# Conv units of a fused causal-convolution and ELU-MLP kernel, rearranged as 64-row tiles in two halves with output rounds in between

## The chip, the cores and the metric

The kernel runs on one core of one Trainium2 chip. Its time is device microseconds of that core, the median of several executions. A ratio is the mean time of one kernel's runs over the mean time of the other's in the same rounds, so it is not quite the ratio of the medians that stand beside it. Intervals are 95% intervals.

Engines are named as the profile does: PE is TensorE's matmul part, PEld its weight load, DVE is VectorE, ACT is ScalarE, POOL is GpSimd.

## The reference, cut to what matters

```python
# x: (8, 4096, 192), weight: (8 heads, 7 taps), moe_w_in: (192, 2048), moe_w_out: (2048, 192)
w   = softmax(weight, axis=-1)                          # per head
att[b, s, h, :] = sum_k w[h, k] * x_pad[b, s + k, h, :] # causal, 24 channels per head
h   = att.reshape(32768, 192) @ moe_w_in
g   = where(h > 0, h, exp(min(h, 0)) - 1)               # ELU
out = g @ moe_w_out
```

## The kernel before: the parts that matter here

32768 tokens are cut into 32 supertiles of 1024 tokens. A supertile has 16 steps; a step ("h" below) computes 128 columns of the hidden layer for 1024 tokens. A half has 8 steps, and it also holds one **conv unit** (four heads of a coming supertile) and 64 **rounds** of the output product of the supertile before. I number the steps of a half 0 to 7.

```python
HALF_STEPS = (10, 10, 6, 6, 10, 11, 11)   # rounds placed behind steps 7, 0, 1, 2, 3, 4, 5 of a half
CONV_AT = ((4, 1, 1), (12, 2, 0))         # a conv unit in step 4 of each half
...
H = psum("H", [P, 3, 2 * GS])             # three slots of two PSUM banks, taken in turn by steps and conv units
ops = psum("ops", [P, 2, GS])             # accumulates the output rounds of a half
...
# TensorE, conv unit m: full-array matmuls, 118 rows of x against a 118 x 112 band of weights
for gr in range(2):
    W(s_x[s % NXB][gr], x_need[s, gr])    # x has landed
W(s_z, z_need[s])
k = slot_of_conv[m]
wait_slot(k)                              # whoever had this slot of H has been read
for q in range(HU):                       # 4 heads
    h = HU * u + q
    ins = pe.matmul(H[0:CW, k % 3, 256 * q : 256 * q + UC],
                    Tm[0:KW, h, :] if s else Tk[0:KW, :, h],
                    xg[0:KW, s % NXB, :, CPH * h : CPH * (h + 1)].rearrange("p w (j i) -> p j w i", j=3),
                    start=True, stop=True)
ins.then_inc(s_cv)
...
# TensorE, a step n: 64-row tiles, three matmuls in each of two row tiles
wait_slot(k)
for j in range(3):
    for r in range(2):
        ins = pe.matmul(H[:, k % 3, GS * r : GS * (r + 1)],
                        w_in[HP * r : HP * (r + 1), j, FC * q : FC * (q + 1)],
                        att[HP * r : HP * (r + 1), s % 2, j, 0:GS],
                        start=(j == 0), stop=(j == 2), tile_position=(HP * r, 0))
ins.then_inc(s_h)
...
# TensorE, a round r: two matmuls, also in 64-row tiles; in the second half of the rounds the
# row tiles swap the two banks of ops (a wait on s_swap stands there)
...
# per step, for each of its two token groups: ScalarE exp(H) -> E; GpSimd clamps E to at most 1;
# VectorE gT = max(E - 1, H), which also frees the slot of H (s_tt)
# ScalarE in the order of the program: exp of step 4, conv eviction, exp of step 5,
# output eviction (ops -> osb, 768 columns), exp of step 6, ...
```

So every step needs a slot of H, and the slot goes round: step n waits until VectorE has finished with what was there three takings ago. In a half the takings are steps 0 to 4, the conv unit, steps 5 to 7. Step 5 therefore takes the slot of step 3, the conv unit that of step 2, and step 7 the conv unit's.

## Time and profile before

| | before |
|---|---|
| time, median of 3 runs | 762.6 us (761.82 to 762.93) |
| span of the profiled execution | 761.0 us |
| a half (8 steps, 1 conv unit, 64 rounds), steady state | 11.287 us |
| start to start of VectorE ops in the steps that wait for it | 0.598 us |

The period of a half is read from the trace: it is the distance between the first w_in matmuls of step 1 in consecutive halves (median over 52 halves; 11.284 to 11.288 in all of them).

From the page of the kernel before, the busy table and the chain of work that ended last:

```profile
PE 749.1 (98%) x11609; PEld 507.6 (67%) x11612; DVE 636.1 (84%) x1033; ACT 639.4 (84%) x1155; POOL 668.8 (88%) x1110
...
PE 95%; DVE 2%; DMA 1%; POOL 1%; ACT 0%; issue 0%; SPq 0%
```

Read alone, these two lines say that TensorE is the limit and nothing else matters. The Trainium skill warns about the first of them (Perfetto Trace Analysis, Tensor Engine Instruction): the end that the profiler gives for a TensorE instruction is estimated, not observed. This trace fits that: almost every w_in matmul is drawn as 376 ns (the rest as 377 to 387) but the next pair starts 216 ns after it, so bars overlap and a matmul that starts 40 or 100 ns late leaves no idle time in the table. Waits of TensorE have to be looked for in the starts.

The timeline of the kernel before, one half, without the other engines' lines (start and duration in us, engine, line, operation, tiles, count). L490 is a step, L519 are rounds, L466 is the conv unit:

```profile
300.26 0.82 PE L490 MATMUL H<-att,w_in 64*128 64x512 bf16 x6
300.92 0.99 PE L519 MATMUL ops<-w_out,gT 64*128 64x192 f16 x20
301.74 0.81 PE L490 MATMUL H<-att,w_in 64*128 64x512 bf16 x6
302.39 0.58 PE L519 MATMUL ops<-w_out,gT 64*128 64x192 f16 x10
302.89 0.62 PE L466 MATMUL H<-xg,Tm 118*112 118x240 bf16 x4
303.44 0.67 PE L519 MATMUL ops<-w_out,gT 64*128 64x192 f16 x12
...
304.80 1.09 ACT L373 ACTIVATE E<-H 128x512 f32<-128x512 f32 x2 [0.26 <-PE H L490]
...
305.77 0.82 ACT L354 ACTIVATE osb<-ops 128x768 f32<-128x768 f32 x1
...
306.46 3.10 ACT L373 ACTIVATE E<-H 128x512 f32<-128x512 f32 x6
```

Ten rounds take 301.74 - 300.92 = 0.82 us, so a round takes 82 ns. The five rounds before conv take 302.89 - 302.39 = 0.50 us where five rounds need 0.41, and the four conv matmuls take 303.44 - 302.89 = 0.55 us where four times 101 ns (240 columns, the distance inside the unit) is 0.40. That excess, 0.24 us, is what the change aims at. ScalarE's exponential of step 5 (304.80) waits for TensorE.

The timeline of VectorE alone around step 3 of the same half (window 300.7 to 303.2 us; a row starts with its first instruction that reaches into the window):

```profile
300.12 3.67 DVE L416 SCALAR_TENSOR_TENSOR gT<-E,H 128x512 f16<-128x512 f32 x6
```

Six ops without a gap: five distances of 598 ns and one duration of 0.68 us. The last of them is the second op of step 3. It ends at 303.789 us, and step 5, which takes that slot, starts at 303.950 (all starts and ends to the nanosecond are in the trace): 161 ns later. In steps 1, 2 and 3 the same distance is 57 ns in nearly every half, and never less than 56. So 56 to 57 ns is what a held start looks like, and step 5 had 105 ns to spare.

From the table of waits of the kernel before (from 60 to 740 us; us in total, times, longest):

```profile
DVE gT L416 <- POOL E L323: 78.1, 120, 1.2
ACT E L373 <- PE H L490: 66.9, 181, 0.5
```

ScalarE waits for TensorE in part of the steps.

### The profile page before, as it was taken

To read this page: it belongs to the slowest core of one execution; us is meant where nothing else is said; L and a number is where in the kernel's file an instruction comes from. 1 tells how busy PE (TensorE), PEld (TensorE's weight loads), DVE (VectorE), ACT (ScalarE), POOL (GpSimd) and SP (SyncE) were. 2 spreads that over 40 slices of the span, in tenths; PEclk is the share of its full clock that TensorE was granted. 3 is DMA by queue.
4 is the path that set the end of the run, shared out by engine and by line. 5 is a ranking of instruction groups with operands and counts; after the bars stand their busy time and mean duration, and the time that the engine had idled before them with its cause. 6 is when DMAs were issued, how large, how long until landed. Compare 5 with 4: busy or idle time off the path is not lost.

```text
span 761.0 us, 27449 instructions
## 1 busy us (share of the span) xinstructions
PE 749.1 (98%) x11609; PEld 507.6 (67%) x11612; DVE 636.1 (84%) x1033; ACT 639.4 (84%) x1155; POOL 668.8 (88%) x1110
## 2 busy tenths in 40 slices
PE   8899999999999999999999999999999999999997
PEld 3256666666666666676666666666666666667666
DVE  2588888889889889889888888988988988988993
ACT  1588888888888888888888888888888888888882
POOL 3799999899989999989989999989998999998892
PEclk9999999999999999999999999999999999999999
DMA  5845645424654533555542554442454653353212
GB/s 102 132 58 92 92 59 92 84 51 85 92 64 87 91 53 75 93 77 73 92 65 63 92 92 59 91 89 48 84 92 68 84 91 58 71 92 77 46 44 65
DMA packets 135499, 59.31 MB, mean 78 GB/s; under 512 B 101680, under 2 KB 134576, under 8 KB 135376
## 3 DMA queue, kind: packets, MB, share of 16 engines
q1 hardware_dynamic: 90112, 39.68, 23.5%
q0 software_dynamic: 44992, 17.67, 21.4%
q8 instruction: 91, 1.49, 0.8%
q14 instruction: 32, 0.26, 0.1%
q10 hardware_dynamic: 272, 0.20, 0.1%
HBM read 34.80 MB, written 25.45 MB: 79 GB/s over the span
## 4 chain that ended last, share of the span: by engine, by line
PE 95%; DVE 2%; DMA 1%; POOL 1%; ACT 0%; issue 0%; SPq 0%
PE H L490 44%; PE ops L519 44%; PE H L466 5%; DVE gT L416 1%; PE ops L448 1%; POOL E L323 1%; PE H L519 1%; DMA conv_band<-wprb 1%; DMA wq<-in_weight_dram 0%; DMA Tk<-conv_band 0%; ACT E L373 0%; POOL xg L270 0%; POOL w_out L311 0%; ACT osb L354 0%; DVE osb L427 0%
## 5 line engine op out<-in xcount | busy, mean ns | idle before, releaser
L416 DVE SCALAR_TENSOR_TENSOR gT<-E,H 128x512 f16<-128x512 f32 x1024 | 630.5, 682 | 98.9 <-POOL E L323 91.2
L323 POOL TENSOR_SCALAR E<-E 128x512 f32<-128x512 f32 x1024 | 605.1, 614 | 65.9 <-ACT E L373 63.3
L373 ACT ACTIVATE E<-H 128x512 f32<-128x512 f32 x1024 | 546.1, 604 | 95.7 <-PE H L490 82.1
L519 PEld LDWEIGHTS ops<-w_out,gT 64*128 64x128 f16 x8064 | 342.4, 94 | 114.3 <-ACT osb L354 10.8
L519 PE MATMUL ops<-w_out,gT 64*128 64x192 f16 x8064 | 414.5, 243 | 0.9 <-DVE gT L416 0.9
L490 PE MATMUL H<-att,w_in 64*128 64x512 bf16 x3072 | 407.0, 377 | 2.9 <-DVE gT L416 2.8
L490 PEld LDWEIGHTS H<-att,w_in 64*128 64x128 bf16 x3072 | 129.4, 94 | 105.5 <-DVE gT L416 7.2
L366 ACT ACTIVATE csb<-H 112x960 bf16<-112x960 f32 x63 | 61.4, 974 | 10.2 <-PE H L466 10.2
L270 POOL DMA_DIRECT2D xg<-in_x_dram x65 | 59.4, 914 | 6.0 <-DVE csb L406 5.9
L354 ACT ACTIVATE osb<-ops 128x768 f32<-128x768 f32 x63 | 51.5, 817 | 5.1 <-PE ops L519 5.1
L466 PE MATMUL H<-xg,Tm 118*112 118x240 bf16 x248 | 38.2, 277 | 0.7 <-DVE gT L416 0.6
L466 PEld LDWEIGHTS H<-xg,Tm 118*112 118x112 bf16 x248 | 23.7, 129 | 11.4 <-issue 10.8
L448 PE MATMUL ops<-zw 128*128 128x512 bf16 x89 | 25.3, 423 | 1.9 <-DVE zw L384 1.5
L448 PEld LDWEIGHTS ops<-zw 128*128 128x128 bf16 x92 | 9.0, 108 | 15.8 <-issue 9.2
L406 DVE CAST csb<-H 112x960 bf16<-112x960 f32 x1 | 1.2, 1158 | 10.2 <-PE H L466 10.2
L427 DVE COPY osb<-H 128x384 f32<-128x384 f32 x1 | 0.6, 558 | 8.9 <-PE H L519 8.9
L519 PE MATMUL H<-w_out,gT 64*128 64x192 f16 x128 | 5.6, 243 | 0.1
L519 PEld LDWEIGHTS H<-w_out,gT 64*128 64x128 f16 x128 | 5.2, 94 | 0.3 <-PE H L519 0.3
L302 POOL DMA_DIRECT2D w_in<-w_in x1 | 0.7, 682 | 5.3 <-DMA w_in<-in_moe_w_in_dram 5.3
L346 ACT ACTIVATE osb<-H 128x384 f32<-128x384 f32 x1 | 0.5, 491 | 4.7 <-PE H L519 4.7
L288 POOL DMA_DIRECT2D w_in<-in_moe_w_in_dram x6 | 3.5, 598 | 0.9 <-DMA att<-csb 0.9
L466 PE MATMUL H<-xg,Tk 118*112 118x240 bf16 x8 | 2.0, 394 | 1.7 <-DMA Tk<-conv_band 1.7
(20 smaller groups left out, 12.0 us busy)
## 6 DMA issues: line engine op xcount, KB each, us to landing
out_dram<-osb SPq DMA_DIRECT2D x127, 192.0 KB, 3.7
xg<-in_x_dram POOLq DMA_DIRECT2D x62, 240.0 KB, 5.3
w_in<-in_moe_w_in_dram POOLq DMA_DIRECT2D x6, 128.0 KB, 5.2
w_out<-in_moe_w_out_dram POOLq DMA_DIRECT2D x1, 768.0 KB, 7.9
att<-csb SPq DMA_TRANSPOSE x32, 5.8
xg<-in_x_dram POOLq DMA_DIRECT2D x2, 192.0 KB, 4.6
w_in<-w_in POOLq DMA_DIRECT2D x1, 384.0 KB, 4.8
w_in<-w_in SPq DMA_DIRECT2D x1, 384.0 KB, 4.2
```

Source lines behind the costliest of these rows:

```text
L270: g.dma_start(xg[0:rows, b, 2 * w0 + gr : 2 * w1 : 2, :], src).then_inc(s_x[b][gr], 16)
L288: g.dma_start(w_in[0:HP, j, c0:c1], bass.AP(tensor=moe_w_in.tensor, offset=8 * j * FF + c0, ap=[[CPH * FF, HEADS], [FF, 8], [1, c1 - c0]], ...
L323: g.tensor_scalar(out=E[:, n % NE, u, :], in0=E[:, n % NE, u, :], scalar1=1.0, scalar2=0.0, op0=ALU.min, op1=ALU.max,).then_inc(s_clp)
L354: a.activation(osb[:, b, :, :, :].rearrange("p g k d -> p g (k d)"), ops[:, :, 0 : 2 * D], ACT.Copy,).then_inc(s_oev)
L366: a.activation(*conv_evac(W, m), ACT.Copy).then_inc(s_ce)
L373: a.activation(E[:, n % NE, u, :], H[:, k, GS * u : GS * (u + 1)], ACT.Exp).then_inc(s_exp)
L406: v.tensor_copy(*conv_evac(W, 1)).then_inc(s_cd)
L416: v.scalar_tensor_tensor(out=gT[:, s % NG3, q, u, :], in0=E[:, n % NE, u, :], scalar=1.0, in1=H[:, slot_of_pair[n] % 3, GS * u : GS * (u + ...
L448: pe.matmul(ops[:, 0, :], zw[:, 0:P], zw[:, 0:GS], start=True, stop=True)
L466: ins = pe.matmul(H[0:CW, k % 3, 256 * q : 256 * q + UC], Tm[0:KW, h, :] if s else Tk[0:KW, :, h], xg[0:KW, s % NXB, :, CPH * h : CPH * (h ...
L490: ins = pe.matmul(H[:, k % 3, GS * r : GS * (r + 1)], w_in[HP * r : HP * (r + 1), j, FC * q : FC * (q + 1)], att[HP * r : HP * (r + 1), s ...
L519: ins = pe.matmul(acc[:, g, D * kb : D * (kb + 1)], gT[HP * rt : HP * (rt + 1), t % NG3, q, g, t0 : t0 + P], w_out[HP * rt : HP * (rt + 1) ...
```

## The change

Its intent: the conv matmuls use the whole array, everything around them uses 64-row tiles. If the conv unit runs in 64-row tiles too, TensorE need not change its mode twice a unit. Two row tiles may not access the same PSUM bank at a time (the Trainium skill, TensorEngine Tiling (Array Packing), Gotcha 1), so in the first half of a unit row tile 0 takes two heads and row tile 1 the other two, and in the second half they swap. A wait on TensorE's own semaphore stands between the halves, and four output rounds are put there to hide it.

```diff
+            cuts = (r0, r0 + 3, r0 + 7, r1) if convs else (r0, r1)
+            for part, (a, b) in enumerate(zip(cuts, cuts[1:])):
+                order.append(("o", t, half, a, b))
+                for k, u in convs:
+                    if part < 2:
+                        conv_at(k, u, part)
 ...
+                    if part == 0:
+                        (the waits for the band, x, the zeros and the slot, as before)
+                    else:
+                        if 2 <= m <= 3:
+                            warm(WARM[2])
+                        W(s_cswap, 2 * m + 2)
-                    for q in range(HU):
-                        h = HU * u + q
-                        ins = pe.matmul(H[0:CW, k % 3, 256 * q : 256 * q + UC],
-                            Tm[0:KW, h, :] if s else Tk[0:KW, :, h], xg[0:KW, ...],
-                            start=True, stop=True)
-                    ins.then_inc(s_cv)
+                    for q in range(2):
+                        for rt in range(2):
+                            hq = 2 * (rt ^ part) + q
+                            h = HU * u + hq
+                            rows = slice(HP * rt, HP + (KW - HP) * rt)      # 64 and 54 rows
+                            ins = pe.matmul(H[0:CW, k % 3, 256 * hq : 256 * hq + UC],
+                                Tm[rows, h, :] if s else Tk[rows, :, h], xg[rows, ...],
+                                start=(part == 0 and q == 0), stop=(part == 1 and q == 1),
+                                tile_position=(HP * rt, 0))
+                            if q == 1 and part == 0:
+                                ins.then_inc(s_cswap)
+                            elif q == 1:
+                                ins.then_inc(s_cv)
```

(Calls are drawn together and the arguments of xg are cut; the counts in the other engines' waits on s_cv double.)

More of the change, by code (lines that the diff above doesn't have):

```diff
@@ L84, in bass_lightweight_conv__then__act_elu_kernel, with conv_at @@
     last_slot = None
-    def conv_at(s, g):
-        m = 2 * s + g
-        slot_of_conv[m] = take_slot(("c", m))
-        order.append(("c", m))
-    for g in range(2):
-        conv_at(0, g)
+    def conv_at(s, u, part):
+        m = 2 * s + u
+        if part == 0:
+            slot_of_conv[m] = take_slot(("c", m))
+        order.append(("c", m, part))
+    for part in range(2):
+        for u in range(2):
+            conv_at(0, u, part)
     rounds_at = {}
@@ L109, in bass_lightweight_conv__then__act_elu_kernel @@
         else:
-            convs = [(s + ahead, g) for at, ahead, g in CONV_AT if at == i and n < NP]
-        convs = [(k, g) for k, g in convs if k < NS]
+            convs = [(s + ahead, u) for at, ahead, u in CONV_AT if at == i and n < NP]
+        convs = [(k, u) for k, u in convs if k < NS]
         if n in rounds_at:
@@ L115, in bass_lightweight_conv__then__act_elu_kernel @@
                 last_slot = take_slot(None)
-            mid = (r0 + r1) // 2 if convs else r1
-            order.append(("o", t, half, r0, mid))
-            for k, g in convs:
-                conv_at(k, g)
-            if mid < r1:
-                order.append(("o", t, half, mid, r1))
-        else:
-            for k, g in convs:
-                conv_at(k, g)
+            cuts = (r0, r0 + 3, r0 + 7, r1) if convs else (r0, r1)
[4 more added lines that the diff above has]
+                        conv_at(k, u, part)
+        else:
+            for k, u in convs:
+                for part in range(2):
+                    conv_at(k, u, part)
     band = nc.dram_tensor("conv_band", (P, TW, HEADS), BF16).ap()
@@ L184, in bass_lightweight_conv__then__act_elu_kernel @@
         s_swap = sema("s_swap")
+        s_cswap = sema("s_cswap")
         s_oev = sema("s_oev")
@@ L256, in load_x @@
                 if s >= NXB:
-                    W(s_cv, 2 * (s - NXB) + 2)
+                    W(s_cv, 4 * (s - NXB) + 4)
                 if s == 0 and gr == 0:
@@ L361, in _scalar @@
                 if item[0] == "c":
-                    m = item[1]
-                    if m == 1:
+                    _, m, part = item
+                    if m == 1 or part == 0:
                         continue
-                    W(s_cv, m + 1)
+                    W(s_cv, 2 * m + 2)
                     a.activation(*conv_evac(W, m), ACT.Copy).then_inc(s_ce)
@@ L404, in _vector @@
             ).then_inc(s_set)
-            W(s_cv, 2)
+            W(s_cv, 4)
             v.tensor_copy(*conv_evac(W, 1)).then_inc(s_cd)
@@ L452, in _tensor @@
                 if item[0] == "c":
-                    m = item[1]
+                    _, m, part = item
                     s, u = divmod(m, 2)
-                    if m == 0:
-                        W(s_band, 48)
-                    if m == 2:
-                        W(s_tm, 1)
-                    for gr in range(2):
-                        W(s_x[s % NXB][gr], x_need[s, gr])
-                    W(s_z, z_need[s])
-                    k = slot_of_conv[m]
-                    wait_slot(k)
@@ L464, in _tensor @@
-                    for q in range(HU):
-                        h = HU * u + q
-                        ins = pe.matmul(
-                            H[0:CW, k % 3, 256 * q : 256 * q + UC],
-                            Tm[0:KW, h, :] if s else Tk[0:KW, :, h],
-                            xg[0:KW, s % NXB, :, CPH * h : CPH * (h + 1)].rearrange(
-                                "p w (j i) -> p j w i", j=3
-                            ),
-                            start=True,
-                            stop=True,
-                        )
@@ L475, in _tensor @@
-                    ins.then_inc(s_cv)
+                    k = slot_of_conv[m]
+                    if part == 0:
+                        if m == 0:
+                            W(s_band, 48)
+                        if m == 2:
+                            W(s_tm, 1)
+                        for gr in range(2):
+                            W(s_x[s % NXB][gr], x_need[s, gr])
+                        W(s_z, z_need[s])
+                        wait_slot(k)
+                    else:
+                        if 2 <= m <= 3:
+                            warm(WARM[2])
+                        W(s_cswap, 2 * m + 2)
@@ new lines, in _tensor @@
+                    for q in range(2):
[3 more added lines that the diff above has]
+                            rows = slice(HP * rt, HP + (KW - HP) * rt)
+                            ins = pe.matmul(
+                                H[0:CW, k % 3, 256 * hq : 256 * hq + UC],
+                                Tm[rows, h, :] if s else Tk[rows, :, h],
+                                xg[rows, s % NXB, :, CPH * h : CPH * (h + 1)].rearrange(
+                                    "p w (j i) -> p j w i", j=3
+                                ),
+                                start=(part == 0 and q == 0),
+                                stop=(part == 1 and q == 1),
+                                tile_position=(HP * rt, 0),
+                            )
+                            if q == 1 and part == 0:
+                                ins.then_inc(s_cswap)
+                            elif q == 1:
+                                ins.then_inc(s_cv)
@@ L564, in _sync @@
                 if item[0] == "c":
-                    m = item[1]
+                    _, m, part = item
                     s, u = divmod(m, 2)
+                    if part == 0:
+                        continue
                     if u == 1:
```

## The prediction

> **What bounds it now.** By the table of busy times PE is busy 749 of 761 us; the chain of waits is 95% PE. The timeline is finer. One half of a supertile (8 pair steps, one conv unit) takes 11.286 us, 59 times in the steady state. In steps 1 to 3 of each half the VectorE ops start exactly 598 ns apart, and the first w_in matmul starts 56 ns after the end of the VectorE op that frees its PSUM slot: PE is held there by 40 to 50 ns a step, though it is drawn as busy. From step 4 on PE sets the pace and ScalarE waits for it (66.9 us in the table of waits). So the conv unit, between steps 4 and 5, is on the path, but with limited slack behind it.
>
> **What is removed.** In the timeline's matmul starts, the first conv matmul comes 172 ns after the last round (usual 80), the second after 147 (usual 101), the next round 198 after the last conv matmul (usual 101): 92 + 46 + 97 = 235 ns a unit. The Trainium skill (TensorEngine Tiling (Array Packing), Key Properties) says that changing the tiling mode drains TensorE; the trace agrees in these gaps. Two row tiles run side by side (rounds start in pairs 3 ns apart), so 8 half matmuls are 4 pairs of 101 ns, 404 ns as before. Estimate: 59 x 0.235 = 14 us (1.8%) if all counted.
>
> **What is added.** Four boundaries in place of two (about 10 ns each now), 256 matmuls and weight loads side by side, and the swap wait. The conv's semaphore comes 280 ns after its last matmul's start; four rounds in between give 101 + 330 ns, of which the weight load needs 80 to 160: nearly or quite hidden. The unit ends about when it did, so its eviction does not move.
>
> **How much counts.** Step 5 takes the PSUM slot of step 3, which VectorE frees in its saturated stretch. Step 5's first matmul starts 161 ns after that (minimum 56), so it can come only about 105 ns earlier, not 235. The other 130 ns become a wait of step 5 on VectorE, which also swallows boundaries and a small swap stall. The conv's own slot has 245 ns to spare and is asked for 245 ns earlier: just enough. Following the waits of all engines through with the trace's durations gives 11.28 us a half before and 11.19 after: 59 x 0.095 = 5.6 us. The start loses about 0.3 us: the first conv unit is whole only after six of eight pairs, and two units get two more warm matmuls, mostly inside waits on VectorE.
>
> **Predicted:** 762.6 - 5.6 + 0.3 = 757.3 us, range 753.5 to 760.5. Faster by over 2%: 0.05; within 2%: 0.93; slower by over 2%: 0.02.
>
> **What would show it.** Period of a half 11.19 us. Matmul starts around conv at 80 to 101 ns, no gaps of 170 to 200. Step 5 starts 56 ns after VectorE's op of step 3 in nearly every half; VectorE still 598 ns apart in steps 1 to 3. Idle before the conv's weight loads (10.8 us) gone. Conv eviction within 50 ns of its old place after step 4.
>
> **What would make it wrong.** If step 3's slot comes free earlier than I think, the gain goes towards 14 us (748.5). If the 54-row tile is not in the mode of the 64-row ones, drains double and the kernel gets slower. If the swap wait stalls by over 130 ns a unit, the gain shrinks to zero.

## The result, and the profile after

| | before | after |
|---|---|---|
| time, median of 4 runs each | 762.76 us (761.82 to 764.24) | 758.53 us (757.76 to 759.43) |
| ratio | | 0.9943 (0.9924 to 0.9963) |
| span of the profiled execution | 761.0 us | 756.5 us |
| period of a half, median | 11.287 us | 11.192 us |
| period of a half, mean of 52 | 11.287 us | 11.202 us |
| step 5 starts after VectorE's end of step 3 (median) | 161 ns | 57 ns |

The result is correct. The page of the changed kernel, the same two lines:

```profile
PE 746.0 (99%) x11872; PEld 510.7 (68%) x11872; DVE 636.0 (84%) x1033; ACT 645.8 (85%) x1155; POOL 668.3 (88%) x1110
...
PE 94%; DVE 2%; DMA 2%; POOL 1%; ACT 1%; issue 0%; SPq 0%
```

Nothing in them tells that the limit has moved; TensorE even looks busier. The timeline of the changed kernel does tell it (L508 is a step, L537 are rounds, L480 is a conv half):

```profile
300.27 0.81 PE L508 MATMUL H<-att,w_in 64*128 64x512 bf16 x6
300.92 0.41 PE L537 MATMUL ops<-w_out,gT 64*128 64x192 f16 x6
301.18 0.41 PE L480 MATMUL H<-xg,Tm 64*112 64x240 bf16 x4
301.43 0.50 PE L537 MATMUL ops<-w_out,gT 64*128 64x192 f16 x8
301.76 0.37 PE L480 MATMUL H<-xg,Tm 64*112 64x240 bf16 x4
301.96 0.50 PE L537 MATMUL ops<-w_out,gT 64*128 64x192 f16 x8
302.38 0.82 PE L508 MATMUL H<-att,w_in 64*128 64x512 bf16 x6
...
303.24 1.09 ACT L378 ACTIVATE E<-H 128x512 f32<-128x512 f32 x2
...
304.21 0.82 ACT L359 ACTIVATE osb<-ops 128x768 f32<-128x768 f32 x1
304.58 1.29 DVE L421 SCALAR_TENSOR_TENSOR gT<-E,H 128x512 f16<-128x512 f32 x2 [0.84 <-POOL E L328]
304.90 3.10 ACT L378 ACTIVATE E<-H 128x512 f32<-128x512 f32 x6
...
306.25 6.07 DVE L421 SCALAR_TENSOR_TENSOR gT<-E,H 128x512 f16<-128x512 f32 x10 [0.38 <-POOL E L328]
```

Three rounds take 0.26 us, two conv pairs 0.25, four rounds 0.33 (so the swap wait is hidden), two conv pairs 0.20; the last four rounds take 302.38 - 301.96 = 0.42 us where 0.33 is enough. That excess in front of step 5 is a wait. VectorE alone, again around step 3:

```profile
298.65 3.67 DVE L421 SCALAR_TENSOR_TENSOR gT<-E,H 128x512 f16<-128x512 f32 x6
```

The last of these six ops ends at 302.320 us and step 5 starts at 302.378: it is held. From step 4 to step 5 TensorE now needs 302.38 - 300.27 = 2.11 us, before 303.95 - 301.74 = 2.21 us: 0.10 us less. It saved more than that in matmul time, and lost the rest waiting for VectorE.

One can now read off the loop that sets the period, all from the fences above. Step 5 starts at 302.38; its exponentials at 303.24 (0.86 later); the output eviction behind them on ScalarE at 304.21 (0.97); the exponentials of step 6 at 304.90 (0.69); VectorE's first op of step 6 at 306.25 (1.35, through the clamp on GpSimd). From there VectorE has twelve ops back to back up to step 3 of the next half, eleven distances of 0.598 = 6.58, then its last duration and the held start, 0.68 + 0.06. The sum is 11.19 us, the measured period. TensorE's matmul stream is in this loop only with step 5 itself.

The table of waits of the changed kernel (from 60 to 740 us) shows that ScalarE has less to wait for from TensorE:

```profile
DVE gT L421 <- POOL E L328: 73.6, 121, 1.2
ACT E L378 <- PE H L508: 52.8, 126, 0.5
```

### The profile page after: what moved, and what is told of

It reads as the page before. It is cut to its first block, busy times and chain, and to the rows that moved or that the text cites. A ratio compares the mean times of both kernels' runs of the same rounds, so it can differ in the third digit from the quotient of the medians. Undisturbed runs are those within 1.5% of the kernel's fastest.

```text
span 756.5 us, 27972 instructions
## 1 busy us (share of the span) xinstructions
PE 746.0 (99%) x11872; PEld 510.7 (68%) x11872; DVE 636.0 (84%) x1033; ACT 645.8 (85%) x1155; POOL 668.3 (88%) x1110
## 4 chain that ended last, share of the span: by engine, by line
PE 94%; DVE 2%; DMA 2%; POOL 1%; ACT 1%; issue 0%; SPq 0%
PE H L508 45%; PE ops L537 43%; PE H L480 4%; DVE gT L421 1%; PE ops L453 1%; POOL E L328 1%; PE H L537 1%; DMA conv_band<-wprb 1%; ACT E L378 0%; DMA Tk<-conv_band 0%; DMA wq<-in_weight_dram 0%; POOL xg L275 0%; POOL w_out L316 0%; ACT osb L359 0%; DVE osb L432 0%
## 5 line engine op out<-in xcount | busy, mean ns | idle before, releaser
L537 PE MATMUL ops<-w_out,gT 64*128 64x192 f16 x8064 | 426.0, 243 | 0.9 <-DVE gT L421 0.9
L537 PEld LDWEIGHTS ops<-w_out,gT 64*128 64x128 f16 x8064 | 352.2, 94 | 104.1 <-ACT osb L359 10.7
L508 PE MATMUL H<-att,w_in 64*128 64x512 bf16 x3072 | 408.0, 378 | 1.3 <-DVE gT L421 1.2
L508 PEld LDWEIGHTS H<-att,w_in 64*128 64x128 bf16 x3072 | 127.1, 94 | 108.2 <-DVE gT L421 5.5
L480 PE MATMUL H<-xg,Tm 64*112 64x240 bf16 x496 | 49.6, 272 | 1.0 <-DVE gT L421 0.6
L480 PEld LDWEIGHTS H<-xg,Tm 64*112 64x112 bf16 x496 | 26.0, 126 | 10.2 <-issue 3.3
L537 PE MATMUL H<-w_out,gT 64*128 64x192 f16 x128 | 5.6, 243 | 0.1
L537 PEld LDWEIGHTS H<-w_out,gT 64*128 64x128 f16 x128 | 5.2, 94 | 0.3 <-PE H L537 0.3
L480 PE MATMUL H<-xg,Tk 64*112 64x240 bf16 (+1 forms) x16 | 2.0, 406 | 2.1 <-DMA Tk<-conv_band 2.1
```

The source lines that it names most:

```text
L480: ins = pe.matmul(H[0:CW, k % 3, 256 * hq : 256 * hq + UC], Tm[rows, h, :] if s else Tk[rows, :, h], xg[rows, s % NXB, :, CPH * h : CPH * ...
L508: ins = pe.matmul(H[:, k % 3, GS * r : GS * (r + 1)], w_in[HP * r : HP * (r + 1), j, FC * q : FC * (q + 1)], att[HP * r : HP * (r + 1), s ...
L537: ins = pe.matmul(acc[:, g, D * kb : D * (kb + 1)], gT[HP * rt : HP * (rt + 1), t % NG3, q, g, t0 : t0 + P], w_out[HP * rt : HP * (rt + 1) ...
```

## The experiments

Theory A is the prediction's: the mode changes cost about 0.24 us a unit, and most of what is saved is lost again, because step 5 then waits for the slot that VectorE frees. Theory B, the rival that the page suggests: TensorE is the limit throughout, and the drains were simply worth less than the gaps look. Other rivals stand at the runs. Periods of a half are medians read from the trace as above; where even and odd halves differ both are given.

| run | median us | ratio to before | period of a half, us | result |
|---|---|---|---|---|
| before | 762.2 to 763.0 | 1 | 11.287 | correct |
| after | 758.53 | 0.9943 | 11.192 | correct |
| no_second_part | 759.11 | 0.9956 | 11.192 | wrong |
| halves_adjacent | 766.94 | 1.0057 | 11.339 | correct |
| full_array_split | 777.26 | 1.0195 | 11.533 | correct |
| full_array_earlier | 764.58 | 1.0027 | 11.286 | correct |
| vector_480_after | 748.15 | 0.9807 | 10.999 and 10.985 | wrong |
| vector_480_before | 755.99 | 0.9913 | 11.203 and 11.148 | wrong |
| half_eviction | 751.07 | 0.9840 | 11.071 | wrong |
| shared_eviction | 751.50 | 0.9845 | 11.071 | correct |
| shared_eviction_before | 755.78 | 0.9900 | 11.160 | correct |
| shared_eviction_12_10 | 750.72 | 0.9832 | 10.999 and 11.096 | correct |
| rounds_12_10 | 761.43 | 0.9978 | 11.189 and 11.270 | correct |
| x_waits_early | 749.91 | 0.9820 | 11.000 and 11.054 | correct |

### no_second_part: is TensorE still the limit?

```diff
 # changed kernel; from the second supertile on the second half of a conv unit has no matmuls
-                    for q in range(2):
+                    for q in range(2 if part == 0 or s == 0 else 0):
```

> The changed kernel without the second half of each conv unit from the second supertile on (result wrong on purpose): about 0.2 us of TensorE work less in each of 59 halves. Theory A (the VectorE-bound release of step 3's PSUM slot, not TensorE, now sets when step 5 may start): time stays at 758.5, within 2 us, and the wait in front of step 5 grows by about 0.2 us. Theory B (TensorE at 99% busy is the limit, and the drains were simply smaller than they looked): 12 us less, about 746.5.

Measured: 759.11 us, ratio 0.9956 (0.9941 to 0.9971), the same as the changed kernel's within both intervals, with the same period of 11.192 us. The timeline of this run, where L509 is a step:

```profile
300.97 0.81 PE L509 MATMUL H<-att,w_in 64*128 64x512 bf16 x6
301.62 0.41 PE L538 MATMUL ops<-w_out,gT 64*128 64x192 f16 x6
301.88 0.41 PE L481 MATMUL H<-xg,Tm 64*112 64x240 bf16 x4
302.13 0.82 PE L538 MATMUL ops<-w_out,gT 64*128 64x192 f16 x16
303.07 0.61 PE L509 MATMUL H<-att,w_in 64*128 64x512 bf16 x4
```

The second conv half is gone, and from step 4 to step 5 it is 303.07 - 300.97 = 2.10 us all the same: eight rounds, which need 0.66 us, take 0.94. The chain of work that ended last, on this run's page, now shows what the changed kernel hid:

```profile
PE 54%; DVE 30%; ACT 7%; POOL 4%; issue 4%; DMA 2%; SPq 0%
```

With no more than a wait of 0.1 us in front of step 5 the chain still went down TensorE's back-to-back bars; with 0.3 us it follows the true releaser. Theory B falls: half the conv work of TensorE is worth nothing in the changed kernel.

### halves_adjacent: what if the swap wait is not hidden?

```diff
-            cuts = (r0, r0 + 3, r0 + 7, r1) if convs else (r0, r1)
+            cuts = (r0, r0 + 5, r0 + 5, r1) if convs else (r0, r1)
```

> The changed kernel with both conv halves between rounds 5 and 6, no rounds between them: the swap wait then stalls TensorE by about 0.21 us a unit (semaphore 280 ns after the last matmul's start, against 101). Theory A: 0.1 us or more of that is swallowed by the waits on the slots of steps 2 and 3, which the changed kernel has anyway: about 762.5, as the kernel before. Theory B: all counts, about 771. If there is no stall: 758.5.

Measured: 766.94 us, between the numbers of the two theories, so both expectations missed. In the trace the stall is larger than I had put it: the first pair of the second half starts 354 ns after the last pair of the first (101 without a wait), and the next pair another 146 ns later (101): 298 ns, not 210. The period grew by 11.339 - 11.192 = 0.147 us against the changed kernel. So half of the stall counts and half is swallowed, and here step 5 is no longer held (its distance to VectorE's end is 214 ns). The rounds in between are necessary: without them the change would be slower than the kernel before.

### full_array_split: does a change of mode cost what the gaps show?

```diff
 # kernel before: four full-array matmuls -> two, four rounds, two
-                    for q in range(HU):
+                    for q in (range(HU) if item[2] is None else range(2 * item[2], 2 * item[2] + 2)):
 # (placed with the cuts r0 + 3 and r0 + 7 of the changed kernel; s_cv counts the second part only)
```

> The kernel before, its conv in full-array matmuls as it was, but each unit split in two times two matmuls with four rounds in between: same work, twice the changes of mode. If a pair of changes costs the 235 ns read from the gaps of the kernel before, and TensorE there has no slack after conv: 59 x 0.235 = 14 us more, about 776. If the gaps are only how matmul starts are drawn: about 763.

Measured: 777.26 us, ratio 1.0195 (1.0180 to 1.0210). In the timeline of this run (L493 is a step, L468 the conv matmuls) each group of two conv matmuls stands between gaps like those around the one group of four before:

```profile
307.23 0.81 PE L493 MATMUL H<-att,w_in 64*128 64x512 bf16 x6
307.88 0.41 PE L522 MATMUL ops<-w_out,gT 64*128 64x192 f16 x6
308.22 0.41 PE L468 MATMUL H<-xg,Tm 118*112 118x240 bf16 x2
308.56 0.50 PE L522 MATMUL ops<-w_out,gT 64*128 64x192 f16 x8
309.00 0.41 PE L468 MATMUL H<-xg,Tm 118*112 118x240 bf16 x2
309.34 0.50 PE L522 MATMUL ops<-w_out,gT 64*128 64x192 f16 x8
```

Three rounds and the way into the first group take 308.22 - 307.88 = 0.34 us in place of 0.25, two conv matmuls and the way out 0.34 in place of 0.20. The period grew by 11.533 - 11.287 = 0.246 us a unit. One more entry into and exit from the full-array mode costs 0.246 us where nothing swallows it, and the 0.235 us read from the gaps was nearly right.

### full_array_earlier: or did only the placing of the unit help?

```diff
-            mid = (r0 + r1) // 2 if convs else r1
+            mid = r0 + 3 if convs else r1
```

> The kernel before with the whole conv unit after three rounds of step 4 in place of five, as early as the first half in the changed kernel. Theory A (the gain comes from the missing changes of mode): as before, 762.7 within 1.5 us. Rival (the gain comes from asking earlier for the conv's slot and from the later rounds): about 758.5.

Measured: 764.58 us, ratio 1.0027 (1.0011 to 1.0044): no gain, rather 2 us more than the kernel before. The period is 11.286 us, as before. The difference of the profiled spans, 1.85 us, lies in the start, where the first w_in matmul comes at 23.8 us in place of 22.5 (1.4 us), and in seven halves that the median does not show, one per batch of four supertiles, which are 68 ns longer than the others (0.5 us; they are explained at the end of the next section). The first w_in matmul comes between 21.0 and 23.9 us across the kernels, and what sets it was not looked into; differences of 1 to 2 us between two kernels' totals may come from there, which is why the periods are given beside the times. The rival falls.

### vector_480_after and vector_480_before: is it VectorE?

```diff
 # from the third supertile on; the other 32 columns of gT keep older values
-                        in0=E[:, n % NE, u, :], ... out=gT[:, s % NG3, q, u, :], ...
+                        in0=E[:, n % NE, u, 0:480], ... out=gT[:, s % NG3, q, u, 0:480], ...
```

> The changed kernel with VectorE's ops on 480 of 512 columns from the third supertile on (result wrong on purpose), so 33 ns less in each. TensorE, ScalarE and GpSimd work are untouched. Theory A (VectorE's saturated stretch, through the slot of step 3, sets the pace): the period of a half falls by about 0.2 us to 10.97, the kernel to about 745 (743 to 749). Theory B (TensorE at 99% busy is the limit): 758.5, unchanged.

> The same cut of VectorE's ops in the kernel before. Theory A: TensorE has less to wait for in steps 1 to 3, but its conv drains stay on the path: about 0.11 us a half, about 756; so with a shorter VectorE op the change is worth about 11 us in place of 4. Theory B: 762.5, unchanged.

Measured: 748.15 us for the changed kernel (10.4 us less) and 755.99 us for the kernel before (7.0 us less than the 762.96 us of the same calls). TensorE's instructions are the same, and it is again shown 99% busy, of a span that is 10 us shorter. So the change is worth 755.99 - 748.15 = 7.8 us with the shorter VectorE ops, and 4.2 us with the full ones. This is the slot wait given back. (The two shortened kernels start differently, with the first w_in matmul at 22.9 and 21.0 us. By the mean periods of 52 halves, 11.013 and 11.175 us, the change is worth 0.162 us a half, or 9.6 us in 59 halves, in place of 0.085 us and 5.0 us.) The gain stayed below the 13.5 us that I had expected. The op got 28 ns shorter, not 33 (0.654 us against 0.682; the 33 can be estimated for 32 columns from VectorE's copies of 960 and 384 columns in the trace of the kernel before, 1158 and 558 ns), and the timeline of VectorE in the shortened run of the changed kernel shows the rest:

```profile
302.80 7.02 DVE L422 SCALAR_TENSOR_TENSOR gT<-E,H 128x480 f16<-128x480 f32 x12 [0.37 <-POOL E L328]
```

Twelve ops in 7.02 us, less one duration of 0.65, are eleven distances of 579 ns on average, where 598 - 28 = 570 would be possible. GpSimd's clamps follow each other at 577 ns in this stretch, so the next limit is only some 20 ns below VectorE's pace.

### half_eviction: is ScalarE's output eviction on the loop?

```diff
 # changed kernel, from the second supertile on
-                    ops[:, :, 0 : 2 * D],
+                    ops[:, :, 0:D],          # 384 columns in place of 768; osb accordingly
```

> The changed kernel with ScalarE's output eviction on 384 of 768 columns from the second supertile on (result wrong on purpose); it stands between the exponentials of steps 5 and 6. Theory A: it lies on the loop step 5, exponential, eviction, exponential of step 6, VectorE, slot of step 3, step 5; it is shorter by 0.3 us, of which some 0.1 us counts before TensorE's step 6 becomes the later one: about 753.5. Theory B: 758.5, unchanged.

Measured: 751.07 us, period 11.071 us (0.12 us less a half). The eviction does lie on the loop. The expectation was 2.4 us too high; it had put the gain at 0.1 us a half.

### shared_eviction: a correct kernel that uses this

VectorE is saturated from step 6 to step 3, but it idles before its ops of step 5 (0.84 us in the timeline of the changed kernel). It can take one of the two token groups there.

```diff
+            def evac_second(n_half):                       # VectorE
+                b = n_half % 2
+                W(s_mm2, n_half + 1)
+                W(s_out[b], 32 * (n_half // 2))
+                v.tensor_copy(osb[:, b, 1, :, :].rearrange("p k d -> p (k d)"), ops[:, 1, 0 : 2 * D]).then_inc(s_ov)
 ...
+                if s and n % 8 == 5:                       # before VectorE's ops of step 5
+                    evac_second(2 * (s - 1) + (n % NQ) // 8)
 ...
 # ScalarE evicts group 0 alone; TensorE and the output DMA of group 1 also wait for s_ov
```

> A correct kernel: the changed one, with the output eviction shared out: ScalarE takes the 384 columns of one token group, VectorE the other 384, put before its ops of step 5, where it idles. ScalarE's piece on the loop gets shorter as in the run with half an eviction; VectorE's piece (0.56 us in the last supertile) delays its ops of step 5 by some 0.14 us, which the slot for step 8 just has to spare. About 751; if VectorE's extra work counts in full (0.47 us a half), over 770.

Measured: 751.50 us, ratio 0.9845 (0.9830 to 0.9859), correct. In the timeline of this kernel the two evictions run side by side, and VectorE goes on with step 5 at once:

```profile
301.70 0.56 DVE L420 COPY osb<-ops 128x384 f32<-128x384 f32 x1 [0.42 <-PE ops L551]
301.77 0.50 ACT L360 ACTIVATE osb<-ops 128x384 f32<-128x384 f32 x1
302.18 1.27 DVE L433 SCALAR_TENSOR_TENSOR gT<-E,H 128x512 f16<-128x512 f32 x2
302.35 3.21 ACT L379 ACTIVATE E<-H 128x512 f32<-128x512 f32 x6
```

From the eviction to the exponential of step 6 it is now 0.58 us on ScalarE, of 0.69 before. VectorE's share of busy time rises from 84% to 89%, and the kernel gets 7 us faster: VectorE took work in a stretch in which it had none, so its being the limit elsewhere did no harm.

### shared_eviction_before: does it need the change?

The same edit in the kernel before.

> The same sharing in the kernel before: also there the eviction lies before step 6's exponential, though TensorE's conv drains stay on the path: about 0.11 us a half, about 756. So the change would again be worth some 5 us.

Measured: 755.78 us, ratio 0.9900 (0.9882 to 0.9917). The two edits are nearly independent: with shared eviction the change is worth 755.78 - 751.50 = 4.3 us, without it 4.2 us.

### shared_eviction_12_10 and rounds_12_10: can TensorE's waiting time be filled?

```diff
-HALF_STEPS = (10, 10, 6, 6, 10, 11, 11)
+HALF_STEPS = (10, 10, 6, 6, 10, 12, 10)
```

> The changed kernel with shared eviction, and one round moved from step 5 (11 to 10) to step 4 (11 to 12), into the time in which TensorE waits for step 3's slot. With the shorter eviction TensorE's way from step 5 to step 6 is the later one, and gets 82 ns shorter: about 746 to 747.

> Control: the changed kernel with that round moved alone. Theory A: nothing, 758.5, as ScalarE's eviction still holds back step 6. Theory B (TensorE's order of rounds matters by itself): as much gain as in the run with both.

Both missed. With the round moved alone the kernel got slower than the changed one (761.43 against 758.53 us), and with the shared eviction it gained nothing clear (750.72 against 751.50, intervals overlapping). The periods show what happened: every second half does what was expected (11.189 us, and 10.999 with shared eviction), the others are 81 and 97 ns longer. In those halves of rounds_12_10 TensorE reaches step 5 2.165 us after step 4, in the others 2.102. I had reckoned with the same free time of 0.12 us in all halves. In the trace of the changed kernel the units differ. A unit of the other kind than the one shown above:

```profile
289.08 0.81 PE L508 MATMUL H<-att,w_in 64*128 64x512 bf16 x6
289.73 0.41 PE L537 MATMUL ops<-w_out,gT 64*128 64x192 f16 x6
290.08 0.41 PE L480 MATMUL H<-xg,Tm 64*112 64x240 bf16 x4
290.30 0.53 PE L537 MATMUL ops<-w_out,gT 64*128 64x192 f16 x8
290.63 0.40 PE L480 MATMUL H<-xg,Tm 64*112 64x240 bf16 x4
290.83 0.53 PE L537 MATMUL ops<-w_out,gT 64*128 64x192 f16 x8
291.19 0.82 PE L508 MATMUL H<-att,w_in 64*128 64x512 bf16 x6
```

Here the three rounds before conv take 290.08 - 289.73 = 0.35 us in place of 0.26. This is the unit that has TensorE's waits for the next x in front of the wait for its slot. They have long been met: in the trace the last x has landed at least 2.6 us before the unit starts. The slot was freed 147 ns before it starts, in the other units 55 ns. The gap of about 180 ns in matmul starts that I had ascribed to the change of mode is still there in every second unit, and the last four rounds take 0.36 us of a possible 0.33: only some 30 ns of waiting are left in these halves, not 0.12 us. One round of 82 ns more does not fit.

### x_waits_early: are the waits for x the cause of that gap?

```diff
 # kernel of shared_eviction_12_10; TensorE, in front of step 3 of the half that has the unit
+                    if s and n % NQ == 11 and s + 2 < NS:
+                        for gr in range(2):
+                            W(s_x[s % NXB][gr], x_need[s + 2, gr])
```

> The kernel with shared eviction and the moved round, with TensorE's two waits for the next x moved from the first half of the conv unit to step 3 of the same half, where TensorE waits for VectorE anyway. In the changed kernel every second conv unit (the one with these waits) still starts 180 ns after the last round and leaves the two row tiles some 35 ns out of step; here those waits have long been met. Theory C (the waits themselves make that gap): the 180 ns become about 90 in all units, and the slower of the two kinds of half (11.095 us against 10.998) becomes as fast: 3 us less, about 748. If the gap has another cause: 750.7, and the gap stays.

Measured: 749.91 us, ratio 0.9820 (0.9805 to 0.9835), correct. The gap of 180 to 190 ns fell to 83 ns in those units, except in every fourth supertile, where the wait for a batch's zero rows still stands there. So the waits for x have part in it. The slower half went from 11.096 to 11.054 us, less than half of the way. The time against shared_eviction_12_10 (750.72 us) is not separable from noise. The traces show how the waits make the gap: it is a wait for the slot. In all nine kernels with three rounds before the unit and the waits in front of it this unit starts 146 to 149 ns after the end of the VectorE op that frees its slot, whatever the gap (medians of 117 to 191 ns, and up to 339 ns where VectorE frees the slot late). A held start without these waits in front comes 54 to 58 ns after (in the changed kernel the other units and steps 2, 3 and 5). In halves_adjacent, where five rounds stand before the unit and not three, the slot has been free for 209 ns when TensorE gets there, and the same waits made no gap (82 ns). And in x_waits_early the delay moved along with the waits: step 3, itself held, starts 147 ns after its slot is free in these halves, in place of 58, and in every fourth supertile the wait for the zero rows alone keeps the unit at 147 ns. So waits that are long met, put in front of a held start, made it some 90 ns later; how much of the missing 55 ns of the slower half comes from step 3 was not tested.

This last kernel and shared_eviction are both faster than the kernel before and the changed one; the gain that is clear of noise is the shared eviction's.

## Why the prediction was right

The measured time, 758.53 us, lies in the range of 753.5 to 760.5, 1.2 us above the 757.3 predicted, and in the class that was given 0.93. Point by point:

- **TensorE is held by VectorE in steps 1 to 3 though it is drawn as busy.** Right, and it was the reading that mattered: the distance of 57 ns there and of 161 ns in front of step 5 gave the limit of the gain. vector_480_before shows it on the chip: 28 ns less per VectorE op took 7.0 us from a kernel whose TensorE was 98% busy.
- **The drains cost 235 ns a unit.** Right in sum: one more pair of changes costs 246 ns (full_array_split). The Trainium skill (TensorEngine Tiling (Array Packing), Key Properties) says that changing the mode drains TensorE; the run agrees and gives the size.
- **Only about 105 of these 235 ns count, because step 5 then waits for the slot of step 3.** Right. Step 5 is held in every steady half (57 ns), the period fell by 95 ns as predicted (11.192 us, 11.19 predicted), and taking out another 0.2 us of TensorE work changed nothing (no_second_part). The wait itself is shorter than the predicted 130 ns: about 0.09 us in one kind of half and 0.03 us in the other, as the conv unit's own wait for its slot takes part of it.
- **The swap wait is hidden by four rounds.** Right: they take 0.33 us in the changed kernel. What they hide is larger than I thought, 298 ns and not about 210 (halves_adjacent).
- **The conv unit's own slot is just free in time.** Half right: the unit starts 55 ns after VectorE's end of step 2 in every second half, so it is held there, by some 10 ns. In the others it is held by some 100 ns: it starts 147 ns after, behind its waits for x.
- **No gaps of 170 to 200 ns remain, and the conv matmuls follow at 101 ns.** Wrong in part. A gap of about 180 ns remains in every second unit, which waits for its slot behind the waits for x, and the second pair of a unit comes 147 ns after the first where the two row tiles are in step (unit 27 of the trace, for instance). Both were swallowed by the wait in front of step 5, as the prediction had said of boundaries in general.
- **The idle time before the conv's weight loads goes.** Mostly: the lines of the conv's weight loads in the page show 10.8 us before and 3.3 us after for the cause "issue".
- **The conv eviction keeps its place within 50 ns.** Wrong: it starts 1.920 us after step 4 in one kind of half and 1.985 us in the other (medians), before it was 1.824. It has no bearing on the time: in no_second_part it is back at 1.824 and the period is the same, and step 7, which takes the slot, starts 1.36 us or more after the eviction's end.
- **The start costs 0.3 us.** Right in size, but not where it was put, so in part by luck. The first w_in matmul comes 0.07 us later than before, which is within what the start differs by between kernels. But the second half of the first supertile, from its step 1 to step 1 of the half that follows, takes 12.264 us in place of 12.024: there a conv unit has no rounds between its two parts, and its second part starts 0.32 us after the last pair of the first. The seven other kernels with that unit in two parts of 64-row tiles take 12.259 to 12.272 us; no_second_part, which has neither the swap wait nor the second part in this unit, takes 12.019.

Of the 1.2 us that the prediction was too low, a part is found: in seven halves, one per batch of four supertiles, the period is 11.283 us, 92 ns more than elsewhere. In each of them GpSimd sets the six zero rows of a new batch (a memset of 0.25 us, which is there in both kernels). In both traces the clamps behind the memset come up to 0.16 us later than in other halves, and VectorE's ops that free the slots of steps 2 and 3 some 0.09 us later. Before, step 5 had that much to spare: it starts on time, 66 to 71 ns after VectorE's end in place of 161, and these halves were no longer than the others. In the changed kernel the conv unit and step 5 are held by these very slots, and both start 92 ns later. (In full_array_earlier the gap before the conv unit is 0.27 us in these halves, in place of 0.18, which makes their 68 ns.) No run was made without the memset. It makes 7 x 0.092 = 0.64 us. Another 0.16 us is the kernel before, which took 762.76 us and not 762.6.

## What to carry to other kernels

Before a gain on the busiest engine is counted, look at the next place where that engine takes a buffer from another one, and measure how long the buffer had been free: the gain is no larger than that slack minus the distance at which a held start is seen. A busy table and a chain of waits cannot tell a TensorE that is the limit from one that is held by 50 to 100 ns per step; starts of instructions can, and so can an experiment that takes TensorE work away. Look also at what stands in front of a held start: waits that were long met made it 147 ns in place of 55 from the slot's release to the start here, and each such start on the path pays that. When the limit is a loop through several engines, an engine that is saturated in one stretch may still be the right place for more work in another, as VectorE was for half of the output eviction.

## What the Trainium skill lacked or had wrong

- TensorEngine Tiling (Array Packing), Key Properties: it says that a change of the tiling mode drains TensorE but gives no size. Here entering and leaving the full-array mode once cost 246 ns (full_array_split).
- TensorEngine Tiling (Array Packing), Gotcha 1: it says that software must keep two row tiles out of one PSUM bank, but not what a wait of TensorE on its own matmuls costs. Bare, the swap cost 298 ns (halves_adjacent: 354 and 146 ns in place of 101 and 101); behind four rounds of 82 ns it was hidden.
- TensorE: Matmul & The Clock Gate, Part 3, gives about 4 ns between the starts of packed tiles. That holds in most of these traces (3 to 4 ns, up to 12 behind the other conv units of the changed kernel), but in the units with the waits for x the second pair's tiles start 33 ns apart, and the pairs behind them stayed 33 to 42 ns apart until step 5.
- No page has what waits that have long been met cost in front of a start that is held: with two of them before the wait for its slot a conv unit starts 146 to 149 ns after VectorE's op that frees the slot, without them 54 to 57 ns.
- Perfetto Trace Analysis, Identifying the Most-Contended Engine, says that matmul busy time is not a good measure of how close a kernel is to its roofline, but not that a TensorE drawn as busy can be waiting for another engine: the changed kernel shows TensorE 99% busy, and leaving out 0.2 us of its work in each half changed the time by 0.6 us, within noise.
